# Probabilities of a head pair through DRAM in 5 transfers instead of 10, two constants in shared homes, a new planned order

## The chip, the cores and the metric

The kernel runs on one core of a Trainium2 chip. The time is what the device takes for one execution, in microseconds (us). Before the change the median of three executions was 710.81 us (709.5 to 714.69).

A core has five engines that run side by side, each through its own list of instructions in order: PE (TensorE, the matmuls, with PEld for its weight loads), DVE (VectorE), ACT (ScalarE), POOL (GpSimd) and SP (SyncE), which here only issues DMA transfers. An instruction that has to wait holds everything behind it on its engine. The transfers themselves run on 16 DMA engines that all issuers share.

## The reference, cut to what matters

Local attention with block summaries, and behind it a two-layer network on the result:

```python
k_sum = k.reshape(B, H, nb, 32, D).max(axis=3)          # B, H, S, D = 4, 8, 768, 64
v_sum = v.reshape(B, H, nb, 32, D).mean(axis=3)
scores_l = where(|i - j| < 16, q @ k.T / sqrt(D), -1e9)  # a window around each row
scores_s = q @ k_sum.T / sqrt(D) + log(32)               # 24 block summaries
a = softmax(concat([scores_l, scores_s]))                # a / (sum + 1e-9)
x = (a @ concat([v, v_sum])).reshape(B * S, H * D)
h = x @ w_in                                             # 3072 x 512 @ 512 x 2048
out = (h - tanh(h)) @ w_out                              # 2048 x 512
```

## The kernel before

The 3072 rows are cut into 8 units (`u`) of 384 rows, half a batch each. A unit has 4 head pairs (`p`), a pair has 3 tiles of 128 rows (`i`). Two pairs share a group: one load of V (`load_v`, line 696, ten or so transfers into the tile `vw`) and one copy of the V means (`put_mean`, line 718, two transfers from `mean`) serve both.

For a tile, PE computes the scores into the bank `pS` (`scores`, line 871: three matmuls from unit 2 on); DVE adds the mask and takes the minimum (`min`), ACT takes the exponentials (`exp`), DVE sums and inverts, DVE or ACT multiplies by the inverse (`normal`). There is one bank `pS`, so the next tile's scores wait for the `min` of this one. In units 0 and 1 PE transposes the probabilities. From unit 2 on (`WIDE = 2`) they go another way (`transpose_probs`, line 919): DVE turns blocks of 32x32, each within itself (`p turn`, `prob` to `turned`), SP writes them to a DRAM scratch (`p save`, `turned` to `place`), and SP reads them back in the turned layout (`p load`, `place` to `probT`). When a pair's three tiles are back, PE multiplies them with `vw` (`values`, line 958) into the bank `pX`. There is one `probT` and, from unit 2 on, one `vw`, so the loads of the next pair wait for this pair's `values`, and so do the V loads of the next group.

The network of a unit follows: 16 steps `f`, each `moe_in` (into `pH`, 12 matmuls of 384 columns in units 1 to 7), its nonlinear part on ACT, POOL and DVE (`gt`, `gu`, `gv`, and the split into `gh` and `gl`), and `moe_out` (into `pY`, 9 matmuls of 512 columns). PE mixes these with the attention of later pairs.

The order is not written out. `program` adds every step to a `Plan` with its cost, its engine or engines, and what it reads and writes; `schedule` (line 170) then plays the engines forward with those costs and lets each take the ready step with the highest level, where a level is the longest path behind the step plus two tables of numbers, `BIAS` (by step) and `KB` (by kind). A step with several possible engines leaves its first one by a table `SL`. For SP the plan reckons `ISSUE` = 0.5 us a transfer, and 8 lanes: a transfer waits for the one eight before it. The instructions are then written in that order, and it is fixed.

Two small tiles are touched as well: `blk` (three matrices of 1/32 for the block means, line 454), with a home of its own, and `top` (the largest keys of a block, line 832), a tile of its own beside `th` (its rounded part) and `tl` (the rest).

Of the kernel before, what the change touches and what calls it, by code (L numbers as in the profile page):

```python
# [105 lines left out]
class Plan:  # L106

    SEEN = {PE: 0.2, ACT: 0.16, DVE: 0.13, POOL: 0.1, SP: 0.95}
    ISSUE = 0.5
    QUEUE = 3.0
    AHEAD = 1.1
    LANES = 8
    LARGE, TURN = 1.25, 0.9
# [1118 lines left out]
```

## Time and profile before

| | before |
|---|---|
| median of 3 executions | 710.81 us (709.5 to 714.69) |
| the profiled execution: time | 710.49 us |
| the profiled execution: span on the core | 708.7 us |
| PE busy | 676.0 us (95%) |
| DVE, ACT, POOL busy | 456.8, 487.5, 256.3 us |
| DMA queue of SP | 198520 packets, 69.31 MB |

A line of the timeline gives start, length, engine, operation, output and inputs, the number of instructions run together, and in square brackets how long the engine stood idle before it and what ended that. "issue" there means that the profile shows nothing that it waited for. A wait is put down to the last releaser that the profile knows. SPq is the queue in which SP issues its transfers. The table of windows gives the busy time of each engine in a stretch of the span; PEclk is the granted clock of TensorE, as a share of full speed.

### The profile page before, as it was taken

The numbers are of one execution on the slowest core, as the hardware profiler recorded it, in microseconds if no ns is written. First come the engines' busy times: TensorE is split into PE (matmuls) and PEld (weight loads), VectorE is DVE, ScalarE is ACT, GpSimd is POOL, SyncE is SP. The second block draws the span as 40 slices with busy tenths as digits, with TensorE's granted clock in tenths as the row PEclk, the third lists the DMA queues.
The fourth block names the chain that finished last, engine by engine and source line by source line (L and its number), as shares of the span: only waits on it lengthen the run. The fifth ranks groups of instructions, "written<-read, shape, count | busy, mean of one in ns | idle before, by whom it ended". The sixth has DMA issues, their size and how long they took to land.

```text
span 708.7 us, 12670 instructions
## 1 busy us (share of the span) xinstructions
PE 676.0 (95%) x3881; PEld 558.1 (79%) x3881; DVE 456.8 (64%) x1406; ACT 487.5 (69%) x1412; POOL 256.3 (36%) x316
## 2 busy tenths in 40 slices
PE   7999999999999999999999799899999999999996
PEld 5654545559888889798878788789888997999894
DVE  3989999999887776678476867577666673000000
ACT  2897777879876777767567786477777784445442
POOL 3120000115444334443544334244435544454443
PEclk9999999999999999999999999999999999999999
DMA  9877785724346542434454454332532334001001
GB/s 248 187 235 208 225 216 165 107 47 120 67 94 124 122 120 56 99 82 118 118 110 83 87 133 88 66 83 60 133 71 67 69 90 97 13 1 45 1 1 50
DMA packets 200710, 72.84 MB, mean 103 GB/s; under 512 B 169720, under 2 KB 193976, under 8 KB 200632
## 3 DMA queue, kind: packets, MB, share of 16 engines
q1 hardware_dynamic: 198520, 69.31, 41.8%
q10 hardware_dynamic: 2112, 2.62, 1.2%
q8 instruction: 33, 0.54, 0.3%
q14 instruction: 45, 0.37, 0.2%
HBM read 54.39 MB, written 15.73 MB: 99 GB/s over the span
## 4 chain that ended last, share of the span: by engine, by line
PE 58%; DVE 15%; DMA 11%; SPq 6%; ACT 6%; issue 3%; DVEq 0%; ACTq 0%
PE pY L67 26%; PE pH L67 24%; SPq L67 6%; DMA raw<-in_moe_w_in_dram 3%; PE pS L67 3%; DVE raw L67 3%; PE pX L67 3%; DMA rawq<-in_q_dram 3%; DVE wf L67 3%; ACT prob L67 2%; DVE probw L67 2%; DVE prob L67 2%; DMA raw<-in_moe_w_out_dram 1%; ACT k L67 1%; ACT gu L67 1%
## 5 line engine op out<-in xcount | busy, mean ns | idle before, releaser
L67 PE MATMUL pH<-xh,wf 128*128 128x384 f32 x548 | 186.8, 374 | 0.1
L67 PE MATMUL pY<-wf,gh 128*128 128x512 f32 x432 | 177.6, 438 | 1.4 <-DVE gh L67 1.4
L67 POOL TENSOR_TENSOR gl<-gv,gh 128x384 fp32r<-128x384 f32 x99 | 102.8, 1039 | 193.0 <-ACT gh L67 157.5
L67 POOL TENSOR_TENSOR gv<-gu,gt 128x384 f32<-128x384 f32 x112 | 117.0, 1045 | 71.9 <-ACT gu L67 54.4
L67 ACT ACTIVATE gt<-pH 128x384 f32<-128x384 f32 x128 | 62.0, 484 | 82.9 <-PE pH L67 74.9
L67 PEld LDWEIGHTS pH<-xh,wf 128*128 128x128 f32 x548 | 102.5, 189 | 19.0 <-DVE wf L67 2.0
L67 ACT ACTIVATE prob<-prob,stats 128x182 f32<-128x182 f32 x183 | 79.9, 441 | 34.6 <-DVE stats L67 34.2
L67 PEld LDWEIGHTS pY<-wf,gh 128*128 128x128 f32 x432 | 80.3, 189 | 25.6 <-issue 11.7
L67 PE MATMUL pH<-xh,wh 128*128 128x384 f32 x252 | 86.7, 344 | 0.0
L67 PE MATMUL pH<-xl,wh 128*128 128x384 f32 x252 | 85.5, 339 | 0.0
L67 PE MATMUL pY<-wh,gh 128*128 128x512 f32 x189 | 76.6, 405 | 1.6 <-ACT tmp L67 1.6
L67 PE MATMUL pY<-wh,gl 128*128 128x512 f32 x189 | 74.4, 394 | 0.0
L67 ACT ACTIVATE gh<-gv 128x384 fp32r<-128x384 f32 x112 | 58.1, 519 | 22.9 <-PE pY L67 22.5
L67 ACT ACTIVATE gu<-gu 128x384 f32<-128x384 f32 x128 | 66.7, 522 | 1.9
L67 ACT ACTIVATE gu<-pH 128x384 f32<-128x384 f32 x128 | 61.8, 483 | 4.9 <-PE pH L67 2.7
L67 DVE CUSTOM_DVE_ANT_0 prob<-pS,mask 128x182 f32<-128x182 f32 x144 | 46.1, 342 | 21.2 <-PE pS L67 19.3
L67 PEld LDWEIGHTS pH<-xh,wh 128*128 128x128 f32 x252 | 47.4, 188 | 2.2 <-issue 0.2
L67 PE MATMUL pS<-k,q 128*128 128x364 f32 (+1 forms) x176 | 44.8, 336 | 4.5 <-DVE stats L67 4.5
L67 PEld LDWEIGHTS pH<-xl,wh 128*128 128x128 f32 x252 | 47.2, 187 | 0.0
L67 DVE STREAM_TRANSPOSE turned<-prob 128x384 f32<-128x384 f32 x72 | 41.2, 574 | 4.4 <-ACT prob L67 2.6
L67 PEld LDWEIGHTS pS<-k,q 128*128 128x128 f32 x176 | 31.4, 190 | 15.5 <-issue 7.5
L67 DVE TENSOR_TENSOR k<-raw,k 64x384 fp32r<-64x384 f32 x96 | 42.5, 482 | 1.2 <-ACT k L67 0.2
(176 smaller groups left out, 1311.6 us busy)
## 6 DMA issues: line engine op xcount, KB each, us to landing
place<-turned SPq DMA_DIRECT2D x144, 64.0 KB
probT<-place SPq DMA_DIRECT2D x96, 96.0 KB
raw<-in_moe_w_out_dram SPq DMA_DIRECT2D x16, 512.0 KB
raw<-in_moe_w_in_dram SPq DMA_DIRECT2D x14, 512.0 KB
out_dram<-tmp SPq DMA_DIRECT2D x23, 256.0 KB
rawq<-in_q_dram SPq DMA_DIRECT2D x96, 48.0 KB
raw<-in_k_dram SPq DMA_DIRECT2D x48, 96.0 KB
vw<-in_v_dram SPq DMA_DIRECT2D x40, 96.0 KB
```

The lines of the kernel that those rows point to most:

```text
L67: return lambda *args, **kwargs: self._tc.keep_in_program_order(op(*args, **kwargs))
```

## The change

- **The way through DRAM.** `turned` now holds the three tiles of a pair, in one buffer instead of two buffers of one tile. The `p turn` of each tile stays. The saves are issued after the third: four transfers of 32 partitions, 96 KB each, with rows of 768 bytes, where there were two for each tile (64 partitions, 64 KB, rows of 256 bytes). `place` has the layout of `probT`, and one transfer of 384 KB loads it back, with 3072 bytes a partition, where there were four of 96 KB with rows of 768 bytes. A pair has 5 transfers where it had 10: 120 in the program where there were 240. The first `p turn` of the next pair must wait until the four saves have read `turned`.
- **Homes.** `blk` is made in the home of `vacc` (a tile used later), `top` in the home of `tl`.
- **Plan.** `ISSUE` is 0.58 instead of 0.5, a weight load counts 1.2 times its bytes, and the tables `BIAS`, `SL` and `KB` have other numbers, so that the order is another on every engine and some steps run on another one. Of the `normal` steps from unit 2 on, DVE has 142 where it had 105, and ACT 2 where it had 39; `gl` is made by POOL 109 times where it was 99, by DVE 3 where it was 13. PE has the same matmuls, and two more of those that only keep it busy in the first 100 us (30 for 28).

```diff
-    ISSUE = 0.5
+    ISSUE = 0.58
...
+        moved = nbytes / rate * (1.2 if kind == "w load" else 1.0)
...
-    fixed(("blk",), [P, 3, NB])
+    buf(("blk",), "vacc", [P, 3, NB])
...
-        if whole:
-            top = th
-        else:
-            top = buf(("top", b, p), "top", [P, PG * NB])
+        top = th if whole else tl
...
-            turned, pt, place = ("tp", u, p, i), ("pt", u, p), ("pd", u, p)
-            buf(turned, "turned", [P, 6, 2, 32], F32, 2)
+            turned, pt, place = ("tp", u, p), ("pt", u, p), ("pd", u, p)
             if i == 0:
+                buf(turned, "turned", [P, 6, NT, 2, 32])
                 share(pt, "probT whole", 1, lambda n: made[("probT",)])
                 buf(place, "place", [P, 4, 2 * NT * 32], F32, 2, scratch)
-            do("p turn", DVE, 0.5, lambda: vector.transpose(at(turned).rearrange("p b a j -> p a b j"), ...), r=..., w=[(turned, 0)])
-            for half in range(2):
-                rows = slice(64 * half, 64 * half + 64)
-                dma("p save", lambda e, half=half, rows=rows: e.dma_start(at(place)[rows, :, 64 * i:64 * i + 64], at(turned)[rows, 2 * half:2 * half + 4].rearrange("p b a j -> p b (a j)")), 64 * 1024, 256, r=[(turned, 0)], w=[(place, (i, half))])
+            do("p turn", DVE, 0.5, lambda: vector.transpose(at(turned)[:, :, i].rearrange("p b a j -> p a b j"), ...), r=..., w=[(turned, i)])
             if i == NT - 1:
-                for b in range(4):
-                    dma("p load", lambda e, b=b: e.dma_start(at(pt)[32 * b:32 * b + 32], at(place).rearrange("(n k) b x -> k b n x", k=32)[:, b]), 32 * 3072, 768, ...)
+                for n in range(4):
+                    def save(e, n=n):
+                        b = 2 * (n // 2)
+                        e.dma_start(at(place).rearrange("(b k) n x -> k b n x", k=32)[:, :, n], at(turned)[32 * n:32 * n + 32, b:b + 4].rearrange("p b i a j -> p b (i a j)"))
+                    dma("p save", save, 32 * 3072, 768, r=[(turned, m) for m in range(NT)], w=[(place, n)])
+                dma("p load", lambda e: e.dma_start(at(pt), at(place)), P * 3072, 3072, r=[(place, n) for n in range(4)], w=[(pt, 0)], before=last)
```

Of the tables one entry of each:

```diff
-KB = {..., ('p save', 2): 627, ...}
+KB = {..., ('p save', 2): 663, ...}
-SL = {..., ('normal', 2, 'vector'): 0.6, ('normal', 2, 'scalar'): 0.6, ...}
+SL = {..., ('normal', 2, 'vector'): 1, ...}
```

Three places of the order, for the prediction. First, SP's list between `values` of pair 1 and `values` of pair 2 in unit 5, where the group changes and `vw` is filled anew (`vw_96` and `vw_95` are that tile). Before:

```order
L67 DMA probT<-place 32x4x192 x2
L67 DMA place<-turned 256x1x64 x2
L67 DMA probT<-place 32x4x192 x2
L67 DMA vw_96<-mean 24x3x256 x2
L67 DMA place<-turned 256x1x64 x2
L67 DMA vw_96<-in_v_dram 64x4x64
L67 DMA vw_96<-in_v_dram 96x4x64
L67 DMA vw_96<-in_v_dram 15x4x64
L67 DMA vw_96<-in_v_dram 64x4x64
L67 DMA vw_96<-in_v_dram 96x4x64
L67 DMA vw_96<-in_v_dram 64x4x64
L67 DMA vw_96<-in_v_dram 32x4x64 x3
```

After, at the same place:

```order
L67 DMA place<-turned 32x4x192 x4
L67 DMA vw_95<-mean 24x3x256 x2
L67 DMA vw_95<-in_v_dram 96x4x64 x2
L67 DMA probT<-place 128x768
L67 DMA vw_95<-in_v_dram 64x4x64 x2
L67 DMA vw_95<-in_v_dram 32x4x64
L67 DMA vw_95<-in_v_dram 64x4x64
L67 DMA vw_95<-in_v_dram 15x4x64
L67 DMA vw_95<-in_v_dram 32x4x64
L67 DMA vw_95<-in_v_dram 64x4x64
L67 DMA vw_95<-in_v_dram 32x4x64
```

Before, eight transfers of the probabilities, four of them saves that wait for DVE, stand among or ahead of the twelve for `vw` (the tenth V load is one row on); now a single `p load` stands among them, and the four saves of the next pair are ahead of all. Between those two `values` PE's list had 36 matmuls into `pH`, 27 into `pY` and 6 into `pS`; it now has 48, 33 and 9.

Second, DVE's list in unit 4 from the third `p turn` of a pair to the first of the next, one of the shortest such stretches of the new order (ISA is `min` and its read of the result). Before, where two buffers served `turned`:

```order
L67 STREAM_TRANSPOSE turned<-prob 128x2x6x32
L67 MEMSET pS 64x15
L67 ISA prob,stats<-pS,mask 128x182
L67 ISA stats 128x1
L67 MEMSET pS 64x15
L67 ISA prob,stats<-pS,mask 128x182
L67 ISA stats 128x1
L67 TENSOR_REDUCE stats<-stats 128x2
L67 RECIPROCAL stats<-stats 128x2
L67 TENSOR_SCALAR prob<-prob,stats 128x182
```

After, from behind the third `p turn` on:

```order
L67 ISA prob,stats<-pS,mask 128x182
L67 ISA stats 128x1
L67 ISA prob,stats<-pS,mask 128x182
L67 ISA stats 128x1
L67 TENSOR_REDUCE stats<-stats 128x2
L67 RECIPROCAL stats<-stats 128x2
L67 TENSOR_SCALAR prob<-prob,stats 128x182 x2
L67 ISA prob,stats<-pS,mask 128x182
L67 ISA stats 128x1
L67 ISA prob,stats<-pS,mask 128x182
L67 ISA stats 128x1
L67 STREAM_TRANSPOSE turned<-prob 128x2x6x32
```

In the new order the `p turn` in the last row waits for the four saves of the pair ahead; the work between is two tiles' `min` and one tile's `normal`. Six of the 23 such stretches of the new order are about this short, the others up to twice as long or more.

Third, DVE's list where the keys of batch 3 are turned (`raw` holds a pair's keys as loaded, two turns of four). Before:

```order
L67 TENSOR_SCALAR prob<-prob,stats 128x182
L67 STREAM_TRANSPOSE turned<-prob 128x2x6x32
L67 STREAM_TRANSPOSE raw<-raw 128x768
L67 TENSOR_REDUCE top<-raw 128x24
L67 ISA prob,stats<-pS,mask 128x182
L67 ISA stats 128x1
```

After:

```order
L67 STREAM_TRANSPOSE turned<-prob 128x2x6x32
L67 SCALAR_TENSOR_TENSOR q_1297<-rawq_93,q_1197 64x384
L67 STREAM_TRANSPOSE raw<-raw 128x768
L67 TENSOR_REDUCE tl_4472<-raw 128x24
L67 ISA prob,stats<-pS,mask 128x182
L67 ISA stats 128x1
```

In both, the turn of the keys, which waits for their load, stands ahead of the next tile's `min`.

More of the change, by code (lines that the diff above doesn't have):

```diff
@@ L436, in program @@
     fixed(("small",), [P, 1])
-    ident, mask, blk, ga, small = (made[n,] for n in ("ident", "mask", "blk", "ga", "small"))
+    ident, mask, ga, small = (made[n,] for n in ("ident", "mask", "ga", "small"))
     def make_ident():
@@ L454, in make_blk @@
     def make_blk():
+        blk = at(("blk",))
         gpsimd.memset(blk, 1.0 / 32)
@@ L659, in go @@
             for t in range(3):
-                tensor.matmul(at(ps)[:NB, :HG * D], blk[:, t], x[:, :, t, :D], start=t == 0, stop=t == 2)
+                tensor.matmul(at(ps)[:NB, :HG * D], at(("blk",))[:, t], x[:, :, t, :D], start=t == 0, stop=t == 2)
         either("pair", {POOL: 1.77, DVE: 0.87}, lambda e: e.tensor_tensor(pairs()[0], *pairs(), op=ALU.add), w=[(base, 0)])
@@ L846, in summarize @@
             k_all, kr = block_k[b, p]
-            do("top max", DVE, 0.87, lambda: largest(k_all(), NB, 0), r=kr, w=[(top, (p, 0)), (top, (p, 1))])
-        keys, cs = [(top, (p, n)) for n in range(2)], slice(n, n + NB)
+            do("top max", DVE, 0.87, lambda: largest(k_all(), NB, 0), r=kr, w=[(tl, p)])
+        keys, cs = [(th, (p, n)) for n in range(2)], slice(n, n + NB)
         if whole:
@@ L851, in summarize @@
             return
-        either("top high", {DVE: 0.1, ACT: 0.15}, lambda e: copy(e, at(th)[:, cs], at(top)[:, cs]), r=keys, w=[(th, p)])
-        either("top low", {DVE: 0.1, POOL: 0.25}, lambda e: e.tensor_tensor(at(tl)[:, cs], at(top)[:, cs], at(th)[:, cs].bitcast(F32), op=ALU.subtract), r=[*keys, (th, p)], w=[(tl, p)])
+        either("top high", {DVE: 0.1, ACT: 0.15}, lambda e: copy(e, at(th)[:, cs], at(tl)[:, cs].bitcast(F32)), r=[(tl, p)], w=[(th, p)])
+        either("top low", {DVE: 0.1, POOL: 0.25}, lambda e: e.tensor_tensor(at(tl)[:, cs], at(tl)[:, cs].bitcast(F32), at(th)[:, cs].bitcast(F32), op=ALU.subtract), r=[(th, p)], w=[(tl, p)])
         top_of[b, p] = (th, tl), [[(th, p)], [(tl, p)]], n
@@ L977, in go @@
                         tensor.matmul(at(px)[64 * a:64 * a + 64, c:c + 64], at(vw)[:N2, n, half, 2 * (p % PG) + a, :], turned_of(u, p, n, a, half), start=True, stop=True)
-        do("values", PE, 1.0 if together else 0.45, go, r=([(("pt", u, p), b) for b in range(4)] if u >= WIDE else [(("pt", u, p, n), 0) for n in tiles]) + [key for n in tiles for half in range(2) for key in vw_keys(vw, n, half)], w=[(px, n) for n in tiles])
+        do("values", PE, 1.0 if together else 0.45, go, r=([(("pt", u, p), 0)] if u >= WIDE else [(("pt", u, p, n), 0) for n in tiles]) + [key for n in tiles for half in range(2) for key in vw_keys(vw, n, half)], w=[(px, n) for n in tiles])
     def x_split(u, p):
```

13 lines of the change are left out of this document (6 added, 7 removed).

## The prediction

> **What bounds the kernel now.** First the page: span, busy times, and the chain of work that ended last.
>
> ```profile
> span 708.7 us, 12670 instructions
> PE 676.0 (95%) x3881; PEld 558.1 (79%) x3881; DVE 456.8 (64%) x1406; ACT 487.5 (69%) x1412; POOL 256.3 (36%) x316
> PE 58%; DVE 15%; DMA 11%; SPq 6%; ACT 6%; issue 3%; DVEq 0%; ACTq 0%
> ```
>
> PE is busy for 676.0 of 708.7 us and no other engine comes near, so the kernel is bound by PE, and an edit that leaves the matmuls alone can win at most the 32.7 us in which PE stands. The windows say where those are.
>
> ```profile
> 0.00:140.00 140.00, 128.35 (x613) 75.66 (x614) 121.06 (x366) 101.76 (x288) 16.27 (x50) 0.99 0.80 201
> 140.00:665.00 525.00, 510.50 (x3091) 450.14 (x3090) 335.14 (x1040) 368.15 (x1082) 222.79 (x249) 1.00 0.37 83
> 665.00:709.00 44.00, 37.10 (x181) 32.29 (x179) 0.56 (x2) 17.62 (x43) 17.23 (x17) 0.96 0.06 21
> 385.00:420.00 35.00, 31.43 (x180) 27.79 (x180) 22.91 (x77) 24.30 (x76) 13.90 (x15) 1.00 0.54 118
> 420.00:455.00 35.00, 31.54 (x194) 28.14 (x193) 23.21 (x75) 21.89 (x65) 12.14 (x15) 0.95 0.40 83
> ```
>
> The columns are the stretch, its length, busy time of PE, PEld, DVE, ACT and POOL, the granted clock, the DMA share and GB/s. PE stands 11.65 us up to 140 (the first loads, and the stage in which the weights are converted and DVE is busy 121 of 140), 14.5 us from 140 to 665, and 6.9 us at the end, where only the last stores are left. The transfers that change all lie in the second stretch. So the change itself can win those 14.5 us, and the half-speed clock that shows in one window: 0.05 x 35 = 1.75 us. PE's timeline, read for what stands in brackets, names nearly all of the 14.5:
>
> ```profile
> 217.19 0.92 PE L67 MATMUL pX<-probT,vw 118*64 118x64 f32 x24 [1.19 <-DMA vw<-in_v_dram]
> 247.89 0.50 PE L67 MATMUL pY<-wh,gh 128*128 128x512 f32 x1 [0.74 <-ACT tmp L67]
> 291.82 0.34 PE L67 MATMUL pX<-probT,vw 118*64 118x64 f32 x4 [0.76 <-DMA vw<-in_v_dram]
> 292.81 0.58 PE L67 MATMUL pX<-probT,vw 118*64 118x64 f32 x12 [0.66 <-DMA vw<-in_v_dram]
> 337.31 0.50 PE L67 MATMUL pY<-wh,gh 128*128 128x512 f32 x1 [0.51 <-ACT tmp L67]
> 362.51 0.34 PE L67 MATMUL pX<-probT,vw 118*64 118x64 f32 x4 [1.03 <-DMA vw<-mean]
> 393.15 0.50 PE L67 MATMUL pS<-k,q 128*128 128x364 f32 x2 [3.35 <-DVE stats L67]
> 446.03 1.55 PE L67 MATMUL pX<-probT,vw 118*64 118x64 f32 x24 [3.46 <-issue]
> 599.13 1.00 PE L67 MATMUL pX<-probT,vw 118*64 118x64 f32 x24 [1.68 <-DMA vw<-in_v_dram]
> ```
>
> Six of these nine are `values` (`pX`) of the pair after a change of group, 8.8 us together: PE waits for V or its means, not for the probabilities. (At 446.03 no releaser is named; SP's queue below shows that the V loads came last.) Why V is late, SP's queue shows, here from the `values` of unit 5, pair 1, which PE runs from 428.08 to 429.00, to that of pair 2:
>
> ```profile
> 428.08 0.92 PE L67 MATMUL pX<-probT,vw 118*64 118x64 f32 x24
> 429.44 0.79 SPq L67 DMA_DIRECT2D probT<-place  x2
> 432.09 1.18 SPq L67 DMA_DIRECT2D place<-turned  x2
> 433.31 1.40 SPq L67 DMA_DIRECT2D probT<-place  x2
> 434.76 1.77 SPq L67 DMA_DIRECT2D vw<-mean  x2
> 436.63 1.21 SPq L67 DMA_DIRECT2D place<-turned  x2
> 437.89 6.11 SPq L67 DMA_DIRECT2D vw<-in_v_dram  x10
> ...
> 431.48 0.58 DVE L67 STREAM_TRANSPOSE turned<-prob 128x384 f32<-128x384 f32 x1
> ```
>
> `vw` is free at 429.00, yet its V loads begin at 437.89: eight transfers of the probabilities go first, and the save at 432.09 waits for a turn that DVE ends at 432.06, with everything behind it. The last V load is issued by 444.00 and PE goes on at 446.03: 2.03 us from issue to use. The wait at 393.15 is another matter:
>
> ```profile
> 385.61 2.25 SPq L67 DMA_DIRECT2D raw<-in_k_dram  x4
> 390.06 1.22 SPq L67 DMA_DIRECT2D place<-turned  x2
> 385.15 0.58 DVE L67 STREAM_TRANSPOSE turned<-prob 128x384 f32<-128x384 f32 x1
> 390.50 0.98 DVE L67 STREAM_TRANSPOSE raw<-raw 128x768 f32<-128x768 f32 x1 [4.77 <-DMA raw<-in_k_dram]
> ```
>
> DVE stands 4.77 us for keys whose load SP has only just issued, the next `min` stands behind that, and PE behind the one bank `pS`: of 4.77 us on DVE 3.35 reach PE, 0.7 of it.
>
> **The change part by part.** The sum is made against the profiled execution, 710.49 us for a span of 708.7; the median of the runs is 0.3 us higher.
>
> *Fewer transfers.* What SP spends on one:
>
> ```profile
> L67 SPq DMA_DIRECT2D place<-turned x144: 507/589/2235, 152.4 to 598.1; - x144
> L67 SPq DMA_DIRECT2D probT<-place x96: 310/430/1805, 163.5 to 601.8; - x96
> ```
>
> A pair takes 6 x 0.589 + 4 x 0.430 = 5.25 us of the queue. A new save has the shape of an old load (32x4x192), so 0.43 us is its lower end and the old save's 0.589 the upper; the new load, 128 rows, I put at 0.43. That is 2.15 to 2.8 us a pair, 59 to 74 us less in 24 pairs. SP's queue is not full, so this counts only where PE waits for something behind it: at the changes of group. In unit 5 the new list has the saves ahead of `values`, then two copies of the means (1.77), ten V loads (6.11) and one load of the probabilities (0.43): 8.3 us from 429.0, and 2.03 to land, 439.3. PE had work until 446.03 - 3.46 = 442.57, and the new order puts more matmuls there. So the 3.46 goes, and the same holds in unit 7 (599.13), where the new list has no save among the V loads either: -1.68. With 446.03 goes the half-speed stretch, -1.75: it shows only in the window of the longest wait. Together -6.9. In units 2 and 3 (217.19, 291.82, 292.81) one bundle of four saves still stands ahead of the last V loads and can hold them until DVE has turned; of 2.61 I take half, -1.3 (ends 0 and -2.6). The 1.03 at 362.51 is the copy of the means, which in the new list stands behind a bundle of saves and three loads of keys; I leave it.
>
> [...]
>
> *The late keys.* DVE's new list still turns keys ahead of the next `min`, behind a load that SP issues in a run of eight instead of four. Whether the load is early enough the order cannot tell: of 3.35 I take half, -1.7 (ends 0 and -3.35). The two waits for `tmp` (1.25) depend on when the output is stored; half, -0.6.
>
> *One buffer for three tiles.* This is the added wait. The first `p turn` of a pair now waits on DVE for the four saves of the pair before: 4 x 0.43 to 4 x 0.589, and 2.03 to land, 3.8 to 4.4 us after the third turn, if SP issues them at once. Behind the waiting turn stand the `min` of the next tile, and PE's scores behind those. What covers it is DVE's work between the two turns, priced by these rows:
>
> ```profile
> L67 DVE CUSTOM_DVE_ANT_0 prob<-pS,mask 128x182 f32<-128x182 f32 x144 | 46.1, 342 | 21.2 <-PE pS L67 19.3
> L67 ACT ACTIVATE prob<-prob,stats 128x182 f32<-128x182 f32 x183 | 79.9, 441 | 34.6 <-DVE stats L67 34.2
> L67 DVE TENSOR_SCALAR prob<-prob,stats 128x182 f32<-128x182 f32 x105 | 41.0, 420 | 1.3
> L67 DVE TENSOR_TENSOR gl<-gv,gh 128x384 fp32r<-128x384 f32 x13 | 9.3, 717 | 49.4 <-ACT gh L67 48.4 <-issue 0.9
> L67 DVE DVE_READ_ACCUMULATOR2_ANT stats<- 128x1 f32 x192 | 15.8, 82 | 0.0
> L67 ACT ACTIVATION_READ_ACCUMULATOR prob<-prob,stats 128x1 f32 x144 | 27.2, 189 | 0.0
> L67 DVE TENSOR_REDUCE stats<-stats 128x2 f32<-128x4 f32 x96 | 14.5, 151 | 26.9 <-ACT prob L67 26.0 <-ACT probw L67 0.2
> L67 DVE RECIPROCAL stats<-stats 128x2 f32<-128x2 f32 x96 | 15.3, 159 | 1.6
> ```
>
> In the shortest stretches that is four `min` (1.37), two `normal` (0.84) and, between the second `min` and the sum, the two exponentials on ACT (0.88); with four reads on DVE (0.33), two on ACT (0.38), the sum and the inverse (0.31) 4.1 us: just covered. SP need not be prompt: at 385.73 a turn ended and its save was issued at 390.06, 4.3 us later, behind keys and queries. Ends: 0, and six short stretches x 4.3 x 0.7 = 18 us. I take two of the six with 1 us each: 2 x 0.7 = +1.4, near the lower end, since the other seventeen stretches are longer and the turn of 431.48 was followed by its save within 0.03 us.
>
> *Work between engines.* DVE gets 37 `normal` x 0.42 = 15.5 us and loses 10 `gl` x 0.717 = 7.2: +8.3 beside the 190 us in which it stands between 140 and 665. ACT is relieved. On the path 0; were DVE full, up to +8.3. The turns themselves, the homes of `blk` and `top`, and two more idle matmuls: 0, since PE's first scores wait for the first keys and queries either way. For the new order up to 140 us I have no row that speaks for a gain or a loss: 0, within 3 either way.
>
> Sum: 710.5 - 6.9 - 1.3 - 1.7 - 0.6 + 1.4 = 701.4.
>
> **Rivals.** *All waits go.* The 14.5 and the 1.75 vanish: 694.2. For it: nine short waits, most with one cause. Against: every fixed order has some wait where a load is later than planned, and the early stage must not lose.
>
> *Hidden anyway.* The ten transfers were not what `values` waited for: the loads at 429.44 and 433.31 had landed long before 446.03. If the new order, with its own late means and keys, brings new waits of the same size, about the 1.75 and a little remain: 707 to 713, no change. For it: 14.5 us is what the order before had left too. Against: at 446.03 and 599.13 the saves stand in the way by name.
>
> *The single buffer holds DVE (slower).* If SP is late with the bundle as at 390.06, DVE waits w at each of the 23 borders between pairs, and 0.7 of it reaches PE: 16.1 w. With the 10.5 won kept, 700 + 16.1 w passes 717.9 from w = 1.1 us; w = 1.3 gives 721. For it: four saves instead of two have to land, all after the third turn. Against: the stretches are longer than 4 us in most places.
>
> [...] No row here has a transfer's own time.
>
> **How the numbers follow.** 1% of 710.8 is 7.1, about what a measurement of this kernel tells from no change: faster is below 703.7, slower above 717.9. The forecast's case runs from 697 to 707 (its ends: late keys and units 2 and 3 all won or not at all, the buffer at 0 or a few us) with a chance of 0.48, 0.36 of it below 703.7; all waits go, 0.12; hidden anyway, 0.25; the buffer, 0.15. So faster 0.36 + 0.12 = 0.48, same 0.12 + 0.25 = 0.37, slower 0.15. The range goes from 691 (all waits gone and 3 us early) to 715: only the buffer's case and a few in a hundred lie outside.
>
> **What would show it.** In the new profile: PE's `pX` rows with no brackets above 1 us in units 5 and 7, the granted clock 1.00 around the middle, V loads in SP's queue right behind the copies of the means; `place` 96 and `probT` 24 times. Wrong would be: DVE rows of `turned` with brackets of a microsecond or more released by a transfer (the single buffer), or PE waiting as long on `stats` or keys as it did on V. PE busy must stay near 676.

## The result, and the profile after

Before, the kernel took 710.15 us (median of 4 executions, 707.69 to 714.69); changed it takes **690.28 us** (median of 4 executions, 689.78 to 690.74). The ratio is 0.9713, with a 95% interval of 0.9663 to 0.9763: 2.9% faster, about 20 us. The forecast was 701.4, so about half of the gain was foreseen.

The page of the changed kernel, its span, busy times and the chain of work that ended last:

```profile
span 689.0 us, 12427 instructions
PE 672.4 (98%) x3885; PEld 556.7 (81%) x3885; DVE 465.5 (68%) x1445; ACT 468.1 (68%) x1355; POOL 270.8 (39%) x334
PE 80%; DVE 11%; DMA 4%; ACT 2%; issue 1%; SPq 1%; POOL 0%; DVEq 0%; ACTq 0%
```

PE's share of the chain went from 58% to 80%, and the shares of DMA and SP's queue together from 17% to 5%. The windows of the changed kernel (the columns as in the prediction):

```profile
0.00:140.00 140.00, 130.74 (x623) 77.11 (x624) 122.30 (x383) 96.37 (x279) 18.32 (x49) 1.00 0.75 197
140.00:665.00 525.00, 524.17 (x3186) 465.29 (x3184) 342.63 (x1061) 364.50 (x1060) 244.44 (x277) 1.00 0.37 85
665.00:709.00 44.00, 17.50 (x80) 14.32 (x79) 0.57 (x2) 7.22 (x17) 8.09 (x8) 0.95 0.06 20
385.00:420.00 35.00, 35.00 (x219) 31.25 (x219) 26.35 (x85) 26.05 (x77) 16.58 (x18) 1.00 0.51 122
420.00:455.00 35.00, 35.00 (x222) 31.77 (x222) 24.98 (x70) 25.02 (x72) 17.12 (x19) 1.00 0.41 87
```

From 140 to 665 us PE stands 0.83 us, where it stood 14.5: 13.7 us less. Up to 140 it stands 9.3 instead of 11.65, 2.4 less. PE's own busy time fell by 3.6 us (676.0 to 672.4), with nearly the same matmuls: 1.75 of it is the half-speed stretch at 446 that is gone (there the granted clock was 0.50 from 446 to 449 us), and as much one in the first 35 us (0.50 from 20 to 22, 0.95 over the window), which this execution didn't have (1.00). The tail gives 0.1: the span ends at 689.0, so 24.0 - 17.5 = 6.5 us idle, and before it ended at 708.7, so 43.7 - 37.1 = 6.6. (The prediction's 6.9 counts up to 709, 0.3 us beyond the span.) Together 13.7 + 2.4 + 3.5 + 0.1 = 19.7, which is what the span lost.

In all of that middle stage PE's timeline has two rows left with a wait of 0.2 us or more:

```profile
252.79 0.49 PE L67 MATMUL pS<-k,q 128*128 128x364 f32 x2 [0.37 <-DVE stats L67]
358.93 0.92 PE L67 MATMUL pX<-probT,vw 118*64 118x64 f32 x24 [0.46 <-DMA vw<-mean]
```

The place that the prediction worked out, in unit 5 between `values` of pair 1 and of pair 2, now reads so on PE and in SP's queue:

```profile
406.79 0.92 PE L67 MATMUL pX<-probT,vw 118*64 118x64 f32 x24
...
405.89 1.77 SPq L67 DMA_DIRECT2D place<-turned  x4
407.71 1.82 SPq L67 DMA_DIRECT2D vw<-mean  x2
409.57 1.03 SPq L67 DMA_DIRECT2D vw<-in_v_dram  x2
410.77 0.35 SPq L67 DMA_DIRECT2D probT<-place  x1
411.16 5.63 SPq L67 DMA_DIRECT2D vw<-in_v_dram  x8
...
425.19 0.92 PE L67 MATMUL pX<-probT,vw 118*64 118x64 f32 x24
```

`vw` is free at 407.71 and the last V load is issued by 416.79: 9.1 us, where it took 15.0. PE has work for 17.5 us between the two, where it had 13.6. So V, with 2.03 us to land, is there 6.4 us early, where it was 3.46 late: 5.9 us of the turn come from the queue and 3.9 from matmuls that the order puts there.

V is not all that came sooner. Waits of DVE for transfers between 140 and 665 us, in total, number and longest; before:

```profile
DVE rawq L67 <- DMA rawq<-in_q_dram: 18.6, 8, 5.3
DVE raw L67 <- DMA raw<-in_k_dram: 10.0, 4, 4.8
```

and after, where none for `raw` (keys) is listed any more:

```profile
DVE rawq L67 <- DMA rawq<-in_q_dram: 1.7, 2, 1.2
```

DVE stood 28.6 us for keys and queries, and stands 1.7.

### The profile page after: what moved, and what is told of

It is laid out like the page before. It is cut to its first block, busy times and chain, and to the rows that moved or that the text cites. A ratio compares the mean times of both kernels' runs of the same rounds, so it can differ in the third digit from the quotient of the medians.

```text
span 689.0 us, 12427 instructions
## 1 busy us (share of the span) xinstructions
PE 672.4 (98%) x3885; PEld 556.7 (81%) x3885; DVE 465.5 (68%) x1445; ACT 468.1 (68%) x1355; POOL 270.8 (39%) x334
## 4 chain that ended last, share of the span: by engine, by line
PE 80%; DVE 11%; DMA 4%; ACT 2%; issue 1%; SPq 1%; POOL 0%; DVEq 0%; ACTq 0%
PE pY L67 37%; PE pH L67 35%; PE pS L67 4%; PE pX L67 3%; DVE wf L67 3%; DVE raw L67 2%; DVE probw L67 2%; DMA rawq<-in_q_dram 1%; DMA raw<-in_moe_w_in_dram 1%; PE pT L67 1%; DMA raw<-in_moe_w_out_dram 1%; SPq L67 1%; DVE gh L67 1%; DMA vw<-mean 0%; DVE stats L67 0%
## 5 line engine op out<-in xcount | busy, mean ns | idle before, releaser
L67 POOL TENSOR_TENSOR gl<-gv,gh 128x384 fp32r<-128x384 f32 x109 | 116.4, 1068 | 165.5 <-ACT gh L67 136.8
L67 PEld LDWEIGHTS pH<-xh,wf 128*128 128x128 f32 x548 | 102.3, 188 | 23.7 <-DVE wf L67 2.8
L67 ACT ACTIVATE prob<-prob,stats 128x182 f32<-128x182 f32 x146 | 64.1, 443 | 16.2 <-DVE stats L67 15.6
L67 DVE TENSOR_SCALAR prob<-prob,stats 128x182 f32<-128x182 f32 x142 | 53.4, 408 | 0.9
L67 DVE TENSOR_TENSOR k<-raw,k 64x384 fp32r<-64x384 f32 x96 | 48.4, 542 | 0.8
```

Of the source, the lines that this page charges most:

```text
L67: return lambda *args, **kwargs: self._tc.keep_in_program_order(op(*args, **kwargs))
```

## Experiments

Two theories. **Transfers:** what the probabilities' transfers take of SP's queue delays V, keys and queries; fewer of them is the gain. **Plan:** the new order is the gain, and with it the number of transfers would matter little. A rival of the prediction is tested beside them: the single `turned` buffer that holds DVE.

### The new order with more transfers

`new_order_10` keeps the changed kernel's order on every engine and issues 10 transfers a pair again, within the same steps: two of the four saves in two pieces each, the load in four.

```diff
-                        e.dma_start(to, x)
+                        for c in (range(0, 4, 2) if n % 2 == 0 else [0]):
+                            d = 2 if n % 2 == 0 else 4
+                            e.dma_start(to[:, c:c + d], x[:, c:c + d])
...
-                dma("p load", lambda e: e.dma_start(at(pt), at(place)), ...)
+                dma("p load", lambda e: [e.dma_start(at(pt)[32 * m:32 * m + 32], at(place)[32 * m:32 * m + 32]) for m in range(4)], ...)
```

(`to` and `x` are the two sides of the save.)

> The kernel after, the same order on every engine, with a pair's four saves issued as six transfers and its one load as four: 10 transfers a pair as before the change, all bytes moved. Transfers: about 2.5 to 3 us more queue a pair, waits come back at the changes of group, 696 to 702. Plan: no change, 689 to 692.

Measured: 699.9 us (697.92 to 703.13, ratio to before 0.9838, interval 0.9791 to 0.9885), 9.6 us more than the changed kernel in the same order; the two intervals of the ratio do not meet. Its window of the middle stage:

```profile
140.00:665.00 525.00, 519.32 (x3153) 459.65 (x3153) 343.67 (x1060) 361.22 (x1051) 241.04 (x274) 1.00 0.37 84
```

PE stands 5.7 us there instead of 0.8, at the same granted clock and the same share of the DMA engines. (The profiled execution is the fastest of the four, 697.92 us. Its span is 7.2 us longer than the changed kernel's; 4.9 of that stand in this stage, 0.7 before it and 1.5 behind.) Where it comes from is plain at the first change of group, in unit 2. SP's queue and PE in the changed kernel:

```profile
206.29 0.34 SPq L67 DMA_DIRECT2D probT<-place  x1
...
214.03 1.90 SPq L67 DMA_DIRECT2D place<-turned  x4
215.97 0.45 SPq L67 DMA_DIRECT2D vw<-in_v_dram  x1
...
220.03 0.92 PE L67 MATMUL pX<-probT,vw 118*64 118x64 f32 x24
```

and with ten transfers:

```profile
205.83 1.72 SPq L67 DMA_DIRECT2D probT<-place  x4
...
216.07 2.87 SPq L67 DMA_DIRECT2D place<-turned  x6
218.98 0.43 SPq L67 DMA_DIRECT2D vw<-in_v_dram  x1
...
221.38 0.92 PE L67 MATMUL pX<-probT,vw 118*64 118x64 f32 x24 [1.74 <-DMA vw<-in_v_dram]
```

From the load of the probabilities to the last V load go 9.68 us in the one and 13.15 in the other; 1.38 of the 3.47 are the three more loads, 0.97 the two more saves, and 1.10 the nine V loads between them, which are the same but took 6.11 us instead of 5.01. With ten, PE goes on 1.97 us after that V load is issued, having waited 1.74; with five the V load has landed by 218.5 (reckoned with the prediction's 2.03 us after its end) and PE, which comes at 220.03, doesn't notice it.

`new_order_16` goes further: three times as many saves, each with rows of 256 bytes, and four loads.

```diff
-                        e.dma_start(to, x)
+                        for c in range(0, 2 * NT * 32, 64):
+                            e.dma_start(to[:, :, c:c + 64], x[:, :, c:c + 64])
```

> The kernel after, the same order, with each save issued as three transfers with rows of 256 bytes and the load as four: 16 a pair. Transfers: 700 to 710. The single buffer (held until 12 transfers have landed, some 9 us after the third turn instead of 4) should now hold DVE: rows of turned with waits of 1 to 4 us released by a transfer, and 0.7 of them on PE. Plan: 690 to 694.

Measured: 728.53 us (726.62 to 731.48, ratio 1.0238, interval 1.0191 to 1.0286), slower than before, and by more than the transfers theory had expected. Middle window:

```profile
140.00:665.00 525.00, 501.29 (x3011) 441.62 (x3011) 337.80 (x1060) 349.29 (x1017) 227.06 (x262) 0.98 0.39 84
```

23.7 us idle, and half-speed stretches (0.89 granted from 290 to 320 us, 0.94 from 210 to 240). Besides V, it is the queries that come late here. The timeline shows twelve saves ahead of them in SP's queue, then the wait on DVE and the one on PE:

```profile
472.68 6.77 SPq L67 DMA_DIRECT2D place<-turned  x12
...
480.15 1.40 SPq L67 DMA_DIRECT2D rawq<-in_q_dram  x3
...
485.72 0.58 DVE L67 STREAM_TRANSPOSE rawq<-rawq 128x384 f32<-128x384 f32 x1 [3.73 <-DMA rawq<-in_q_dram]
487.42 0.51 PE L67 MATMUL pS<-k,q 128*128 128x364 f32 x2 [3.33 <-DVE stats L67]
...
300.48 0.58 DVE L67 STREAM_TRANSPOSE turned<-prob 128x384 f32<-128x384 f32 x1 [5.04 <-DMA place<-turned]
```

The last row is the single buffer's hold: six waits, 9.4 us, the longest 5.04 (PE's next wait, at 301.57, is for V). So this rival exists, and grows with what stands in the queue: `new_order_10`, with six, has two such waits (1.8 us, the longest 0.9). In the changed kernel no `turned` row waits for a transfer. That is not only because there are four saves: `new_way_old_tables` (below), with four in another order, has three such waits (3.8 us, the longest 1.82), though none of PE's waits of 0.2 us or more follows them.

### A transfer that carries next to nothing

Is it the issuing, or the moving of the same bytes in other pieces? `new_order_small` leaves the five transfers as they are and issues behind each one more, of a single 4 KB piece.

```diff
+    spares = scratch.tile([120, 16, 64], F32, name="spares", bufs=1)
+    number = iter(range(120))
+    def spare(e):
+        e.dma_start(spares[next(number)], q[0, 0, 0:16, :])
...
                         e.dma_start(to, x)
+                        spare(e)
...
-                dma("p load", lambda e: e.dma_start(at(pt), at(place)), ...)
+                dma("p load", lambda e: [e.dma_start(at(pt), at(place)), spare(e)], ...)
```

> The order of after on every engine; behind each of the five transfers of a pair one more is issued, of one piece of 4 KB from q to a place that nobody reads: ten issues a pair, and hardly more data. If each transfer's turn in SP's queue is the price (0.31 us and more each): 694 to 701, PE idle 3 to 6 us between 140 and 665. If it is the moving of the probabilities in more and shorter pieces: 689 to 692, idle under 1.5.

Measured: 708.44 us (10 executions, 706.79 to 711.73; ratio 0.9956, interval 0.9922 to 0.9989). 0.5 MB of added data costs 18 us, more than either theory expected; PE stands 12.4 us between 140 and 665. Its rows in SP's queue:

```profile
L67 SPq DMA_DIRECT2D place<-turned x96: 309/579/1527, 161.9 to 597.4; - x96
L67 SPq DMA_DIRECT2D probT<-place x24: 337/378/1297, 167.6 to 599.6; - x24
L67 SPq DMA_DIRECT2D spares<-in_q_dram x120: 488/495/1762, 162.2 to 599.9; - x120
```

A piece of 4 KB takes 0.495 us of the queue, more than a save of 96 KB in 128 rows took in the changed kernel (0.434), and the saves between them became longer too. None of SP's listed waits is for the small transfers. So it is the turn in the queue that is paid for, and not the moving of the probabilities.

`new_order_tiny` does the same with 128 pieces of 4 bytes (`spares[...]` of 128 x 1 from `q[0, 0, 0:P, 0:1]`).

> The order of after on every engine. Behind each of the five transfers of a pair a sixth to tenth is issued, each of 128 rows of 4 bytes from q to a place that nobody reads: ten issues a pair, but only 2.5 KB more to move. If the number of transfers in SP's queue is what delays V (each issue costs about 0.43 us): 697 to 702, like the run with ten real transfers in this order (699.9), PE idle 4 to 7 us between 140 and 665. If it is the moving of the data in short rows: 690 to 692, idle near 0.8.

Measured: 864.95 to 878.64 us in three executions, and 1690.63 in one, about the time of two programs, which stays unexplained. Neither theory expected anything like it, and it doesn't answer the question, since something else is added. SP's own waits between 140 and 605 us, the first line:

```profile
SPq L67 <- DMA spares<-in_q_dram: 76.4, 33, 4.8
```

Nothing in the kernel reads these pieces, so it is SP's later transfers that wait for them to land; the plan reckons with just that, each transfer waiting for the one eight before it. So these transfers, half a kilobyte each in 4-byte pieces, held the queue in 33 waits of up to 4.8 us, although their issue (a median of 0.497 us) is no longer than that of the single piece (0.495). The 76 us are not the whole of the 175 us that this kernel takes longer; the rest stays open.

### The old order with fewer transfers

`old_order_7b` and `old_order_0b` keep the order of before on every engine. The first leaves out three of a pair's four loads, the second all ten transfers; the steps stay in the plan with their costs. Behind its program this kernel sums the squares of some of its values, and runs a second form of the program where the sum is large. As the probabilities are not all there in these two, that test is set so that it never asks for more.

```diff
-                dma("p save", lambda e, half=half, rows=rows: e.dma_start(...), ...)
+                dma("p save", lambda e: None, ...)
...
-                    dma("p load", lambda e, b=b: e.dma_start(...), ...)
+                    dma("p load", lambda e: None, ...)
...
-        bits = struct.unpack("i", struct.pack("f", SMALL))[0]
+        bits = 0x7FFFFFFF
```

(That is `old_order_0b`; in `old_order_7b` the saves stay, and one load, for `b == 0`.)

> The order of before on every engine. Left out are three of the four loads of a pair (three quarters of the turned probabilities are whatever lay there); the six saves stay: seven transfers a pair. The test of the sum of squares at the end always ends the kernel. If the transfers delay V: 692 to 701, PE idle about 6 us between 140 and 665. If the order alone made the waits: 706 to 712, idle near 14.

> The order of before on every engine, with all ten transfers of a pair left out (the second products get whatever lay in the buffer). The test of the sum of squares at the end always ends the kernel. If the transfers delay V: 682 to 692, PE idle under 2 us between 140 and 665. If the order alone made the waits: 700 or more.

Measured: 696.58 us with seven transfers (695.7 to 697.85, ratio 0.9784, interval 0.9733 to 0.9835) and 690.8 with none (687.62 to 691.3, ratio 0.9684, interval 0.963 to 0.9738). The middle window with seven:

```profile
140.00:665.00 525.00, 517.97 (x3142) 457.99 (x3141) 334.45 (x1031) 372.30 (x1090) 227.53 (x252) 1.00 0.32 70
```

and with none:

```profile
140.00:665.00 525.00, 522.87 (x3170) 462.62 (x3169) 336.10 (x1034) 376.74 (x1101) 228.84 (x256) 1.00 0.21 47
```

14.5 us of idle time become 7.0 and 2.1, in the very order that had them. The old order was able to run at the changed kernel's speed; the transfers of the probabilities kept it from it. Two rivals go with that. The shared homes of `blk` and `top` are not needed for the gain, since both kernels have the homes of before. And the saves that wait for DVE are not what holds V in the main: with seven transfers all six saves are still there, SP waits for `turned` 47.7 us between 140 and 665 (before 36.4), and yet 14.3 of the 20 us are won. The old order with just the five transfers of the change was not run.

The same two had run once with that test as it is, and went on into the second program:

> The kernel before, in its own order, with three of the four loads of a pair left out (three quarters of probT are not loaded, the output is another): 7 transfers a pair, the saves that wait for DVE all still there. Transfers, by their number: about 3 x 0.43 us less queue at each change of group, 704 to 707. If the saves that wait for DVE are what holds V, or if it is the plan: 708 to 711.

> The kernel before, in its own order, with all 240 transfers of the probabilities left out (PE multiplies with what stands in probT, so the output is another). If the transfers in SP's queue made the waits (transfers), the 8.8 us of waits for V, half of the 3.35 for keys and the 1.75 of half clock go: 697 to 700. If it was the order's own placing of loads and reads (plan), most waits stay: 705 to 710.

Their times, 1474.65 and 1456 us, are those of two programs. In the traces the first program has an idle middle of 5.9 and 1.1 us, much like the repeats; nothing else is read from them.

### Time in SP's queue against time of the kernel

What these runs vary can be put in one number: the number of a kernel's transfers of probabilities times the median that each takes in SP's queue. The rows of the changed kernel:

```profile
L67 SPq DMA_DIRECT2D place<-turned x96: 309/434/1418, 160.8 to 577.0; - x96
L67 SPq DMA_DIRECT2D probT<-place x24: 338/348/612, 164.2 to 579.0; - x24
```

of `new_order_10`:

```profile
L67 SPq DMA_DIRECT2D place<-turned x144: 309/427/1778, 160.1 to 583.7; - x144
L67 SPq DMA_DIRECT2D probT<-place x96: 313/419/1512, 164.3 to 586.3; - x96
```

of `new_order_16`:

```profile
L67 SPq DMA_DIRECT2D place<-turned x288: 302/430/1515, 153.9 to 614.7; - x144
L67 SPq DMA_DIRECT2D probT<-place x96: 312/420/1772, 166.0 to 617.8; - x96
```

and of `old_order_7b`:

```profile
L67 SPq DMA_DIRECT2D place<-turned x144: 507/606/1598, 150.4 to 586.3; - x144
L67 SPq DMA_DIRECT2D probT<-place x24: 310/332/481, 161.4 to 588.5; - x24
```

| kernel | order | SP's time for them, us | kernel, us |
|---|---|---|---|
| none | before | 0 | 690.8 |
| after | after | 96 x 0.434 + 24 x 0.348 = 50 | 690.3 |
| seven (fewer bytes) | before | 144 x 0.606 + 24 x 0.332 = 95 | 696.6 |
| `new_order_10` | after | 144 x 0.427 + 96 x 0.419 = 102 | 699.9 |
| `new_order_small` | after | 96 x 0.579 + 24 x 0.378 + 120 x 0.495 = 124 | 708.4 |
| before (beside the two of its order) | before | 144 x 0.589 + 96 x 0.430 = 126 | 710.9 |
| `new_order_16` | after | 288 x 0.430 + 96 x 0.420 = 164 | 728.5 |

The two orders lie on one curve, as near as they can be compared; not all rows were measured side by side, and the kernel before took 710.15 to 712.5 us beside them. The first 50 us cost nothing that can be seen, though the rows for 0 and for 50 are of different orders, and from about 100 on nearly half of each further microsecond comes back in the kernel's time (28.6 us for 62 in the new order, 14.3 for 31 in the old). That fits with `new_order_10` being some 11 us faster than before with as many transfers: its saves have 64 or 128 rows and take 0.427 us each, before's have 256 rows and take 0.589.

### Other orders

Does any order do, then? `new_way_old_tables` has the five transfers, with the tables `BIAS`, `SL` and `KB` of before; `old_way_new_tables` has the ten, with the tables and the two costs of after; `new_old_costs` is the changed kernel with the two costs of before. The plan is made anew in each, so each has an order of its own.

```diff
-    ISSUE = 0.58
+    ISSUE = 0.5
...
-        moved = nbytes / rate * (1.2 if kind == "w load" else 1.0)
+        moved = nbytes / rate * 1.0
```

(`new_old_costs`; in the others only the tables are exchanged, and the two costs put in. `old_way_new_tables` has two buffers for `turned`, as before, and not the three that its expectation speaks of.)

> Five transfers a pair and the two shared homes, but the three tables of numbers that steer the planner are those of before, so that the order is a third one. If the transfers are the cause of the gain: 690 to 699, PE idle under 6 us between 140 and 665. If the order that was searched for is the cause: 704 or more, idle above 10.

> Ten transfers a pair as before, three buffers for the turned tiles, but the three tables and the two costs of the planner are those of after. If the transfers are the cause: 700 to 711, PE idle above 6 us between 140 and 665. If the tables are: 690 to 697, idle under 4.

> After, with the planner's two cost numbers put back (an issue at 0.5, weights without the factor 1.2): a fourth order. If the transfers are the cause: 689 to 697. If the order has to be this one: 699 or more.

| | transfers | time, us | ratio to before, interval |
|---|---|---|---|
| `new_way_old_tables` | 5 | 698.35 | 0.9818, 0.9763 to 0.9872 |
| `new_old_costs` | 5 | 704.9 | 0.99, 0.9845 to 0.9955 |
| `old_way_new_tables` | 10 | 704.21 | 0.9893, 0.9839 to 0.9947 |

The first and the third lie where the transfers theory had them. The second lies where the plan theory had it: the same five transfers, and 14.6 us slower than after. In its profile 7.2 us more stand idle between 140 and 665 than after, 2.8 more before 140, and PE is busy 4.7 us longer. PE waits mostly for work of other engines, and once for V (1.32 us, at 296.46). Three of PE's rows, and one of DVE:

```profile
155.50 0.43 PE L67 MATMUL pS<-k,q 128*128 128x364 f32 x1 [1.34 <-DVE k L67]
184.65 0.50 PE L67 MATMUL pY<-wh,gh 128*128 128x512 f32 x1 [1.17 <-ACT tmp L67]
395.50 0.49 PE L67 MATMUL pS<-k,q 128*128 128x364 f32 x2 [1.18 <-DVE stats L67]
...
394.27 0.58 DVE L67 STREAM_TRANSPOSE rawq<-rawq 128x384 f32<-128x384 f32 x1 [3.36 <-DMA rawq<-in_q_dram]
```

The last shows that the wait at 395.50 comes from late queries again, as in the kernel before; at 155.50 it is DVE that has too much to do, with 19.2 us of work from 140 to 160.

The largest wait of `old_way_new_tables` stands in a like place, and ends with DVE again:

```profile
157.08 0.40 PE L67 MATMUL pS<-k,q 128*128 128x364 f32 x1 [3.12 <-DVE stats L67]
```

So an order can throw away what the transfers give. Numbers that suit a kernel do not suit its neighbour: a new way through DRAM with the old tables leaves 8 us, a change of two costs 14.6. The plan theory is right in that much, and wrong in that the order made the gain: the order of before, with none of these transfers in SP's queue, had 20 us in it.

### The first 140 us

To see whether the early 2.4 us are the order's, the kernel before was profiled once more.

> The kernel before, looked at once more. If its order costs the early 2.4 us that it lies behind after by 140 us: PE is busy 128.0 to 128.7 of the first 140 again. If that differs from run to run: 129.5 or more. The waits for V in the middle should come back at the same places, 12 us and more of idle time between 140 and 665.

It took 713.21 us in this one execution, with the same waits for V at the same places (the longest 3.37 us, at 447.99). Its first window:

```profile
0.00:140.00 140.00, 128.34 (x610) 74.71 (x611) 120.44 (x363) 100.72 (x285) 16.30 (x50) 0.99 0.79 200
```

128.34 us busy, as at first (128.35): it repeats. But `old_order_0b`, in the same order, has

```profile
0.00:140.00 140.00, 130.04 (x616) 76.10 (x617) 123.15 (x371) 102.40 (x292) 17.19 (x52) 0.99 0.81 201
```

though the transfers that it leaves out would begin only at about 152 us; and `new_order_small`, in the order of after, has 128.48. So neither the order nor those transfers by themselves explain these 2 us, and they stay open. The half-speed stretch in the first 35 us does not follow the change either: `before`, `before_again` and `old_order_0b` had it (0.95 granted in that window), `old_order_7b`, in the same order and with much the same wait before 18.6 (2.11 us, where the three had 1.98 to 2.02), did not (1.00).

## Why the prediction was right or wrong

**PE bounds the kernel, and its waits come from SP's queue: right.** The saves stand ahead of V, V is used 2.03 us after its issue, and with them out of the way the waits of units 5 and 7 are gone, with the half-speed stretch: -6.9 forecast, and 3.46, 1.68 and 1.75 found. The queue's saving was put at 59 to 74 us; it is 126 - 50 = 76.

**Units 2 and 3: wrong in size.** "Of 2.61 I take half", since a bundle of saves still stands ahead of the last V loads. In unit 2 it does, at 214.03, but takes 1.90 us and waits for no turn; V is in 1.6 us before PE wants it. In unit 3 the bundle takes 1.98 us from 280.66, and by the same reckoning V is in less than 0.2 us before PE, which is close. All 2.61 went. With ten transfers in the same order the waits are back, 1.74 us at 221.38 and 0.97 at 290.29.

**Late keys, means and `tmp`: wrong in size.** Taken were 1.7 of 3.35, none of 1.03, and 0.6 of 1.25; gone are all but the 0.46 for the means and a new 0.37 for `stats`. The step that failed stands, for keys and queries, in the sentence "this counts only where PE waits for something behind it: at the changes of group". Keys and queries are behind the saves as well, DVE is what waits for them (28.6 us, now 1.7), and through the one bank `pS` so does PE. With sixteen transfers a pair DVE's waits for queries come back (27.0 us), and PE's behind them; so do those for `tmp` (2.32 us at 255.18) and for the means (0.91 at 377.29). In the old order with seven transfers the wait for keys was still 3.16 us, with none 0.22 was left.

**One buffer for three tiles: +1.4 forecast, 0 found.** The hold is real (9.4 us of DVE with sixteen transfers a pair), but in this order four saves of 0.434 are off the queue before DVE comes round. SP was not late with them, as had been feared: it stood waiting for the turn in 18 places, 108.9 us in all between 140 and 665. No row of the changed kernel shows what the four saves take to land, and DVE never waited for them.

**The early stage: 0 within 3 forecast, 2.4 found, and 1.75 of clock.** The idle time lies within the stated bound, and its cause stays open. The half-speed stretch was not in the sum at all. That such a stretch costs this kernel its 1.75 us is not shown either: the other three executions of the changed kernel had a lower mean granted clock (0.994 to 0.997, against 0.998 in the profiled one) and took no longer (689.78 to 690.29 us).

Together: 1.3 for V in units 2 and 3, 1.03 for the means, 1.65 and 0.65 for keys and `tmp`, 1.4 for the buffer and 1.1 for waits too short to be named (14.5 less the nine quoted), less the 0.83 that is left, are 6.3; 2.4 and 1.75 for the early stage and 0.1 for the tail make it 10.6. The profiled execution lies 701.4 - 690.7 = 10.7 below the forecast.

**The rivals.** "All waits go" came true, at 694.2 less the early 4: the range's lower end, made of that case and 3 us, was 0.7 us too high. That the end lay so near is partly luck: the waits that the case names went, but the early gain that was added to it as a bound came without a known cause. "Hidden anyway" is refuted by the old order with none. "The single buffer holds DVE" shows with twelve saves a pair (9.4 us on DVE), and in small with fewer; not in the changed kernel. The doubts that the sum had halved one by one fell the same way; time in one queue lies behind most of them.

**What would show it.** `place` 96 and `probT` 24 times, no bracket above 1 us at `pX`, the clock at 1.00 in the middle, and no `turned` row held by a transfer: all as written. PE's busy time, which "must stay near 676", is 672.4: the clock term of the forecast itself should have taken it to 674.3.

## What to carry to other kernels

SP's queue, with its transfers in the order of the list, was here an engine like the others (126 us for the probabilities before, 50 after): add up what the instructions of such a queue take, and ask of every load behind them when it is wanted, not only of those at which the bottleneck is seen to wait. Doubts that hang on one such queue go or stay together, so they should be one case with one chance, not halves of each. And when a step is made cheaper, an order that was planned for the old one has to be planned again; a neighbour's numbers can cost as much as the change brings.

## What the runs showed of the hardware

A transfer's turn in SP's queue did not go by its bytes. The medians were 0.589 us for 64 KB in 256 rows, 0.43 for 96 KB in 128, 0.348 for 384 KB in 128 rows of 3072 bytes, and 0.495 for one piece of 4 KB from DRAM to DRAM. Nor did its shape settle it: the same save took 0.434 in the changed kernel and 0.579 with a small transfer behind each, and the same load 0.430 before and 0.332 where three of four were left out. 128 pieces of 4 bytes cost no more to issue than the one piece (0.497), but landed so late that the queue stood 76 us for them.

The length of a wait did not settle whether the clock went to half. The second profiled execution of the kernel before lost 0.05 of the clock in both of these windows, with a longest wait of 3.27 us in the first and 3.37 in the second:

```profile
385.00:420.00 35.00, 31.73 (x175) 27.94 (x174) 22.05 (x75) 24.31 (x75) 14.15 (x16) 0.95 0.52 113
420.00:455.00 35.00, 31.63 (x194) 28.57 (x194) 22.99 (x69) 21.46 (x63) 11.78 (x14) 0.95 0.43 90
```

In the first execution a wait of 3.35 us in 385 to 420 had left it at 1.00, so the shorter wait cost the clock and the longer one did not. In the other window 3.46 us had cost 0.05, and so did 3.37. In `new_order_16` shorter waits stand ahead of such stretches: between 240 and 290 us its longest wait is 2.32 us, and the granted clock is 0.97; from 385 to 420 it has only two waits, of 0.98 and 0.51 us within 3 us, and behind them the matmuls of 384 columns take 0.52 us each, from 409.26 to 412.14, where they took 0.34 ahead of them. (In the first execution of the kernel before they took 0.52 from 448.00 to 448.96, at a granted clock of 0.50.)

```profile
240.00:290.00 50.00, 47.47 (x278) 42.53 (x277) 41.87 (x133) 36.96 (x113) 19.61 (x29) 0.97 0.55 120
```
